# A Fourier filter beside an MLP mixer: the inverse length-47 set of one pair moved behind the forward set of the next pair

## The chip, the cores and the metric

The kernel runs on one core of one Trainium2 chip. The metric is the device time of one execution in microseconds (us). Three executions of the kernel before took 2443.66, 2444.45 and 2446.20 us; their median is 2444.45 us. All data are float32.

## What is computed

Two blocks follow each other. The first is a Fourier filter along a sequence of 3008 for each of 8 batches and 256 channels; the second is an MLP mixer on its result.

```python
X = np.fft.rfft(x, axis=1)                    # x: (8, 3008, 256)
Y = X * (filt_r + 1j * filt_i)[None]          # filt: (1505, 256)
y = np.fft.irfft(Y, n=3008, axis=1)

h = np.maximum(y.transpose(0, 2, 1) @ w_tok1, 0.0) @ w_tok2   # tokens, inner size 256
u = y + h.transpose(0, 2, 1)
out = u + np.maximum(u @ w_ch1, 0.0) @ w_ch2                  # channels, inner size 1536
```

## The kernel before

**The filter.** A length of 3008 is 64 times 47. The transform is done in two steps: a length-64 step ("a" units, `a_pair`) that writes its result to the DRAM tensor `z_tmp`, and a length-47 step that reads it. The length-47 step goes over 16 *pairs* of residues, numbered c. For each pair it does four things:

- `b_pair(c)`: the forward set. Four matmuls (`four`, L523), each on a 64x64 quarter of the array, from `t2` into the two PSUM banks named `acc` and `b` (the list `turn`). Then VectorE multiplies both banks by the filter (two instructions, L674) into the tiles `p1` and `p2`.
- `join(c)`: VectorE makes the complex product out of them in place in `p1` (L679, L680).
- `bi_pair(c)`: the inverse set. Four more quarter matmuls on L523 read `p1` and write two banks; ScalarE copies both out (`by_block`, L660) into `t3`, and two DMAs of the SyncE queue store it to `g_tmp` (L689).
- the loads of pair c+2 (`t2_load`, `w_load`), issued on the SyncE queue between the first two.

The pools around this: `p1` and `p2` have one buffer each, `t2` and `t3` two, the tables `wb` and the filter tiles three. The PSUM tag `pg` has two banks; every other tag has one.

**The batches.** `GROUPS` is (0), (1, 2), (3, 4), (5, 6), (7). The filter of the first group runs alone at the start. Each later group's filter runs beside the mixer of the group before it: `dft(GROUPS[1])` beside batch 0, `dft(GROUPS[2])` beside batches 1 and 2, and so on. Batch 7's mixer has nothing beside it. A group of two batches streams 512 columns in each quarter matmul, the last group, with one batch, 256.

**The mixer.** Its channel part is cut into 6 column tiles `m` of a batch and 6 inner blocks `jp` of each, together 36 *tiles* to a batch, in the order (m, jp). Both products use seven half-size multiplications instead of eight, so there are many small additions, most of which VectorE does. In each tile TensorE runs, in this order:

- `up_first` (L936): four matmuls into two new `pg` banks. ScalarE copies one quarter out (`s`, L939), then VectorE does `up_middle`: `u2` (written `hh<-ps_pg,s 128x256`) and then two sums into `s` (`s<-ps_pg,hh`).
- `down` part 0 of the tile before (L970, moving operand `hh`): three matmuls into the four `po` banks. Place 0 of the schedule follows.
- `up_last` (L952): three matmuls into the same `pg` banks. VectorE then adds both banks into `hh` (`hh<-ps_pg,s 128x512`, two instructions) and ScalarE applies the ReLU (L957). Place 1 follows.
- `down` part 1 of the tile before (L970, moving operand `t`): four matmuls on the sums t1, t3, t2, t4 in that order. VectorE makes these sums before (`h_sums`: one `t<-hh 128x512`, then two `t<-t,hh 128x256`). With the last `jp` of an m, `finish` is called here: VectorE adds the `po` banks into `u` and `r` over this and the next tiles. Place 2 follows.

Most matmuls are 128x128 by 256 columns. One such matmul is two passes in the profile, and a pass starts 0.216 us after the one before.

**Where the filter's steps go.** `mix` is a generator that stops at the places 0, 1 and 2 of every tile; at each stop the loop at the end of the kernel decides by `due` whether the filter's generator takes its next step. For the groups after the first, a forward set is due at place 1 of `jp` 5 and `jp` 2, `join` at place 1 of `jp` 0 and place 0 of `jp` 3, and an inverse set at place 0 of `jp` 1 and place 2 of `jp` 3. In the last m of a group the forward set is due at `jp` 1 instead of 2. Beside batch 0 there are only 36 tiles, so a forward set is due in most tiles, its `join` at place 2 of the same tile and its inverse set at place 0 of the next.

The order of each engine's instructions is the order in which the program emits them (`manual_schedule`); nothing is reordered later. A new tile in a buffer waits until every reader of the tile before it in that buffer is done.

Of the kernel before, what the change touches and what calls it, by code (L numbers as in the profile page):

```python
# [127 lines left out]
def kernel(  # L128
# [53 lines left out]
    def bank(tag):  # L182
        return (psg if tag == "pg" else psum).tile([P, 512], FP32, tag=tag, name="ps_" + tag)
# [341 lines left out]
    def half_of(half, n=HALF):  # L525
        return slice(half * HALF, half * HALF + n)
# [30 lines left out]
    def dft(bs):  # L557
# [102 lines left out]
            nc.scalar.copy(out=out.rearrange("p b (e g i) -> p b g e i", e=DH, i=CW),  # L660
                           in_=ps.rearrange("p b (g e i) -> p b g e i", e=DH, i=CW))

        def two_banks():
            return [bank(tag).rearrange("p (b d) -> p b d", b=2)[:, 0:nb, :] for tag in turn]

        def b_pair(c):
            pss, wb, t2 = two_banks(), wbs[c], t2s[c]
            four(lambda h, i: pss[h][half_of(i)], lambda h, i: wb[half_of(h, KH), i], lambda h, i: t2[half_of(h, KH), i])  # L670
            where = (p1p, p2p)
            for h in range(2):
                prods[c, h] = where[h].tile([P, 2, nb, D], FP32, tag="p%d" % (h + 1), name="p%d" % (h + 1))
                nc.vector.tensor_tensor(out=prods[c, h], in0=pss[h].unsqueeze(1).to_broadcast([P, 2, nb, D]),  # L674
                                        in1=filts[c % FB][:, :, 0, :].unsqueeze(2).to_broadcast([P, 2, nb, D]), op=ALU.mult)
# [3 lines left out]
            nc.vector.tensor_tensor(out=p1[:, 0], in0=p1[:, 0], in1=p2[:, 1], op=ALU.subtract)  # L679
            nc.vector.tensor_tensor(out=p1[:, 1], in0=p1[:, 1], in1=p2[:, 0], op=ALU.add)  # L680

        def bi_pair(c):
            pss, wb, p = two_banks(), wbs[c], prods.pop((c, 0))
            four(lambda i, h: pss[i][half_of(h)], lambda i, h: wb[half_of(i), 2 + h], lambda i, h: p[half_of(i), h])
            t3 = t3p.tile([P, KC, nb, D], FP32, tag="t3", name="t3")
            for i in range(KC):
                by_block(t3[:, i], pss[i])
            for h in range(2):
                nc.sync.dma_start(g_d[place_of[bs[0]][0]][ts(c, KC), ts(h, KH)].rearrange("k r b d -> r k b d"),  # L689
                                    t3[half_of(h, KH)])  # L690
# [8 lines left out]
        yield "w"  # L699
        yield "b"  # L700
        if not first:
            for c in range(K2 // KC):
                b_pair(c)
                if c + 2 < K2 // KC:
                    t2_load(c + 2)
                    w_load(c + 2)
                yield "m"
                join(c)
                yield "i"
                bi_pair(c)  # L710
                if c + 1 < K2 // KC:
                    yield "b"
            return
        if first:
            for i in range(2):
# [243 lines left out]
    def down(m, jp, part, hh, t, po):  # L959
        hw = width(m) // 2  # L960
        if not po:
            for i in range(4):
                po.append(bank("po%d" % i).rearrange("p (s n) -> p s n", s=2))
        b11, b21, b22 = (hh[:, i, 0:hw] for i in (0, 3, 2))
        t1, t3, t2, t4_ = (t[:, i, 0:hw] for i in range(4))

        todo = (((0, 0, 1, 0, 1, b21), (0, 1, 0, 1, 2, b22), (2, 0, 1, 0, 0, b11)),
                ((1, 1, 1, 0, 6, t1), (3, 0, 1, 1, 4, t3), (2, 1, 0, 1, 5, t2), (1, 0, 0, 1, 3, t4_)))
        for i, j, first, last, n, mov in todo[part]:
            nc.tensor.matmul(po[i][:, j, 0:hw], chan[1][:, jp, n, :], mov, start=(jp == 0 and first == 1),  # L970
                             stop=(jp == JP - 1 and last == 1))
# [74 lines left out]
    def mix(next_ready):  # L1046
# [31 lines left out]
        for i in range(len(items) + 1):  # L1078
# [50 lines left out]
            loads(b)  # L1129
            yield b, i % n, 1  # L1130
            if old:
                down(mo, jo, 1, hhs.pop(i - 1), tts.pop(i - 1), pos[bo, mo])
                if jo == JP - 1:
                    todo_v.extend(finish(bo, mo, uts[bo, mo], pos[bo, mo]))
                    one_step()
                    one_step()
# [16 lines left out]
    with tc.manual_schedule():  # L1153
# [70 lines left out]
        for b, i, place in mix(next_ready):  # L1224
            if group + 1 < len(GROUPS) and b == GROUPS[group + 1][0]:
                if not done:
                    raise AssertionError("the filter's steps don't fit beside the mixer's")
                group += 1
                done = group + 1 == len(GROUPS)
                todo = iter(()) if done else dft(GROUPS[group + 1]) if group else second  # L1230
                coming = "a"
            if done:
                continue
            jp = i % JP
            if coming in "aw":
                due = place == 1 or group == 0
            elif group:
                due = (jp, place) in {"b": ((5, 1), (1 if i >= n - JP else 2, 1)), "m": ((0, 1), (3, 0)), "i": ((1, 0), (3, 2))}[coming]
            else:
                due = (jp - (coming == "i")) % JP in ((5, 1, 2, 3) if i < 4 * JP else (5, 0, 1, 2, 3)) and place == {"b": 1, "m": 2, "i": 0}[coming]  # L1240
            if coming == "a" and group == 0 and i < JP - 1:
                due = (2, 0, 1)[place]
            for _ in range(due):
                if not done:
                    coming = next(todo, "end")
                    done = coming == "end"
# [30 lines left out]
```

## Time and profile before

The profiled execution took 2445.61 us, of which 2443.8 us are its span.

| what | value |
|---|---|
| median of three runs | 2444.45 us |
| profiled execution, span | 2445.61 us, 2443.8 us |
| TensorE granted clock, mean | 0.995 |
| VectorE, ScalarE, GpSimdE busy | 79%, 28%, 25% of the span |
| quarter matmuls on L523, forward and inverse sets | 128 sets: 96 of 512 columns, 32 of 256 |
| first forward set, last inverse set start at | 226.5 us, 2076.3 us |

The trace gives each instruction's start and duration from the span's start. A timeline row can hold several instructions of one kind: "x8" are eight, and the duration is then that of all of them together. A row of `L523` with `<-t` is part of a forward set, with `<-p` part of an inverse set. In square brackets stands how long the engine idled before the row and what ended the idling.

### The profile page before, as it was taken

How to read it: one execution, taken by the hardware profiler on the slowest of the kernel's cores; microseconds unless marked ns; L12 is line 12 of the kernel's file. 1: busy time of each engine (PE TensorE's matmuls, PEld its weight loads, DVE VectorE, ACT ScalarE, POOL GpSimd, SP SyncE). 2: the span in 40 equal slices, each digit the busy share in tenths (PEclk: the TensorE clock that was granted, in tenths of full speed). 3: DMA queues.
4: the chain of work that ended last, by engine and by line, in shares of the span. 5: the costliest groups of instructions: out<-in, count | busy, mean ns of one | idle time of the engine just before them, and what ended most of it. 6: DMA issues, size and time to landing. Idle time of an engine off the chain costs nothing.

```text
span 2443.8 us, 35574 instructions
## 1 busy us (share of the span) xinstructions
PE 2399.8 (98%) x12340; PEld 1971.9 (81%) x12340; DVE 1937.0 (79%) x3684; ACT 687.0 (28%) x1355; POOL 621.0 (25%) x1115
## 2 busy tenths in 40 slices
PE   7999999999999999999999999999999999999998
PEld 4666676978788877987888878897889888898887
DVE  7798788787887788778878887877787787777776
ACT  5733223132222222123222222213221222212222
POOL 7476332122112211211211122112112112112121
PEclk8999999999999999999999999999999999999999
DMA  9985446453352222445344322433324121411100
GB/s 215 249 231 170 147 148 180 157 160 108 113 150 90 74 86 79 158 128 158 97 118 122 87 81 73 156 96 118 101 78 149 50 72 47 148 62 31 38 15 20
DMA packets 187419, 278.65 MB, mean 114 GB/s; under 512 B 35485, under 2 KB 125291, under 8 KB 187240
## 3 DMA queue, kind: packets, MB, share of 16 engines
q1 hardware_dynamic: 140952, 212.56, 29.1%
q0 software_dynamic: 34688, 53.83, 8.2%
q10 hardware_dynamic: 11600, 10.00, 1.3%
q8 instruction: 98, 1.61, 0.3%
q14 instruction: 81, 0.66, 0.1%
HBM read 193.52 MB, written 82.72 MB: 113 GB/s over the span
## 4 chain that ended last, share of the span: by engine, by line
PE 88%; DVE 6%; DMA 3%; issue 1%; ACT 1%; POOL 0%; SPq 0%; ACTq 0%; DVEq 0%; POOLq 0%
PE ps_po L970 33%; PE ps_pg L936 18%; PE ps_pg L952 14%; PE ps_b L523 5%; PE ps_b L802 3%; PE ps_acc L857 3%; PE ps_acc L802 2%; PE ps_b L857 2%; PE ps_b L835 2%; PE ps_acc L835 2%; DVE t L914 1%; PE ps_acc L523 1%; PE ps_b L751 1%; DVE hh L914 1%; DMA st<-in_moe_w_tok_dram 1%
## 5 line engine op out<-in xcount | busy, mean ns | idle before, releaser
L1017 POOL DMA_DIRECT2D out_dram<-r x752 | 408.2, 550 | 1636.0 <-ACT hh L957 1157.1
L914 DVE TENSOR_TENSOR hh<-ps_pg,s 128x512 f32<-128x512 f32 (+3 forms) x864 | 481.6, 585 | 230.7 <-ACT s L939 227.9
L957 ACT ACTIVATE hh<-hh 128x512 f32<-128x512 f32 (+1 forms) x576 | 347.7, 621 | 951.0 <-DVE hh L914 947.1
L970 PE MATMUL ps_po<-t,wc 128*128 128x256 f32 (+1 forms) x2304 | 546.8, 380 | 5.0 <-DVE t L914 4.0
L970 PEld LDWEIGHTS ps_po<-t,wc 128*128 128x128 f32 x2304 | 426.4, 190 | 130.9 <-DVE t L914 45.1
L970 PE MATMUL ps_po<-hh,wc 128*128 128x256 f32 (+1 forms) x1728 | 414.0, 375 | 1.4 <-POOL wc L382 0.8
L936 PE MATMUL ps_pg<-v,wc 128*128 128x256 f32 (+1 forms) x1728 | 413.4, 375 | 0.2 <-DVE v L914 0.2
L970 PEld LDWEIGHTS ps_po<-hh,wc 128*128 128x128 f32 x1728 | 326.5, 190 | 42.9 <-ACT s L939 3.4
L936 PEld LDWEIGHTS ps_pg<-v,wc 128*128 128x128 f32 x1728 | 326.8, 190 | 40.9 <-DVE v L914 3.2
L952 PE MATMUL ps_pg<-u,wc 128*128 128x256 f32 (+1 forms) x1152 | 295.2, 379 | 0.6 <-DVE hh L914 0.4
L952 PEld LDWEIGHTS ps_pg<-u,wc 128*128 128x128 f32 x1152 | 214.9, 190 | 57.5 <-DVE hh L914 25.8
L914 DVE TENSOR_TENSOR t<-t,hh 128x256 f32<-128x256 f32 (+1 forms) x576 | 244.9, 425 | 19.8
L914 DVE TENSOR_TENSOR s<-ps_pg,hh 128x512 f32<-128x512 f32 (+1 forms) x288 | 196.0, 681 | 30.7 <-DVE hh L914 0.9
L939 ACT COPY s<-ps_pg 128x256 f32<-128x256 f32 (+1 forms) x288 | 105.9, 368 | 335.5 <-PE ps_pg L936 332.5
L914 DVE TENSOR_TENSOR t<-hh 128x512 f32<-128x512 f32 (+1 forms) x288 | 194.0, 674 | 0.6 <-ACT hh L957 0.6
L936 PE MATMUL ps_pg<-u,wc 128*128 128x256 f32 (+1 forms) x576 | 171.8, 380 | 3.4 <-DVE hh L914 3.4
L952 PE MATMUL ps_pg<-v,wc 128*128 128x256 f32 (+1 forms) x576 | 168.8, 375 | 0.0
L936 PEld LDWEIGHTS ps_pg<-u,wc 128*128 128x128 f32 x576 | 106.2, 190 | 35.1 <-DVE hh L914 20.1
L914 DVE TENSOR_TENSOR u<-ps_acc,u 128x256 f32<-128x256 f32 (+1 forms) x84 | 46.2, 549 | 94.0 <-PE ps_acc L857 86.6
L952 PEld LDWEIGHTS ps_pg<-v,wc 128*128 128x128 f32 x576 | 109.2, 190 | 12.6
L914 DVE TENSOR_TENSOR u<-ps_b,u 128x512 f32<-128x512 f32 (+2 forms) x126 | 74.4, 591 | 28.9 <-PE ps_b L857 26.7
L857 PE MATMUL ps_acc<-w 128*128 128x256 f32 (+1 forms) x336 | 85.2, 376 | 0.0
(149 smaller groups left out, 2718.0 us busy)
## 6 DMA issues: line engine op xcount, KB each, us to landing
w<-w_tmp SPq DMA_DIRECT2D x84, 448.0 KB
w<-w_tmp SPq DMA_DIRECT2D x35, 896.0 KB
out_dram<-r POOLq DMA_DIRECT2D x696, 32.0 KB, 3.3
t<-g_tmp SPq DMA_DIRECT2D x42, 512.0 KB
g_tmp<-t SPq DMA_DIRECT2D x96, 192.0 KB
t<-z_tmp SPq DMA_DIRECT2D x180, 96.0 KB
z_tmp<-t SPq DMA_DIRECT2D x60, 256.0 KB
filt<-in_x_dram SPq DMA_DIRECT2D x90, 128.0 KB
```

Of the source, the lines that this page charges most:

```text
L523: nc.tensor.matmul(outs(i, j), stat(i, j), mov(i, j), start=True, stop=True)
L751: nc.tensor.matmul(acc[:, t, :], w1[:, a, ts(t, P)], t4[b, a // TC4][:, a % TC4, :], start=(a == 0 and t == 0), stop=(a == A - 1 and t == ...
L802: nc.tensor.matmul(ps[:, at], w[:, n], mov, start=(j == 0 and i in (0, 2)), stop=(j == AP - 1 and i >= 5))
L835: nc.tensor.matmul(ps[:, ds(q * P, n)], t4[b, c][:, r, ts(dh, P)], wai[:, 0:n], start=(first and q == 0), stop=(not first and q == 3))
L857: nc.tensor.matmul(ps[:, ds(j * hw, hw)], h1[:, n, :], w2m[m % 2][:, at, 0:hw], start=(i < 2 and j == 0), stop=(j == len(todo) - 1))
L914: nc.vector.tensor_tensor(out=out, in0=in0, in1=in1, op=op)
L936: nc.tensor.matmul(ps[:, 0:hw], chan[0][:, jp, n, :], mov, start=True, stop=True)
L939: nc.scalar.copy(out=s[:, 0], in_=g[0][:, 0, 0:hw])
L952: nc.tensor.matmul(ps[:, 0:hw], chan[0][:, jp, n, :], mov, start=True, stop=True)
L957: nc.scalar.activation(out=hs, in_=hs, func=AF.Relu)
L970: nc.tensor.matmul(po[i][:, j, 0:hw], chan[1][:, jp, n, :], mov, start=(jp == 0 and first == 1), stop=(jp == JP - 1 and last == 1))
L1017: q.dma_start(bass.AP(tensor=ob.tensor, offset=ob.offset + row * D + g * cw, ap=[[N1 * D, 32], [D if h else -D, n], [1, cw]]), blocks[ts(g ...
```

## The change

A forward set is now followed at once by the inverse set of the pair before, and both stand in the middle of `down` part 1 rather than ahead of it. The inverse set takes the two `pg` banks (those of the tile's own up product) instead of `acc` and `b`. Only the last inverse set of a group stays on its own, at its old place and in its old banks. `down` part 1 is split into two parts of two matmuls, with a new place 1.5 between them. The filter's VectorE multiplication is split off into `products` and is emitted behind the inverse set.

```diff
-        def two_banks():
-            return [bank(tag).rearrange("p (b d) -> p b d", b=2)[:, 0:nb, :] for tag in turn]
+        def two_banks(tags):
+            return [bank(tag).rearrange("p (b d) -> p b d", b=2)[:, 0:nb, :] for tag in tags]
...
         def b_pair(c):
-            pss, wb, t2 = two_banks(), wbs[c], t2s[c]
+            pss, wb, t2 = two_banks(turn), wbs[c], t2s[c]
             four(lambda h, i: pss[h][half_of(i)], lambda h, i: wb[half_of(h, KH), i], lambda h, i: t2[half_of(h, KH), i])
+            return pss
+
+        def products(c, pss):
             where = (p1p, p2p)
...
-        def bi_pair(c):
-            pss, wb, p = two_banks(), wbs[c], prods.pop((c, 0))
+        def bi_pair(c, tags):
+            pss, wb, p = two_banks(tags), wbs[c], prods.pop((c, 0))
...
-            for c in range(K2 // KC):
-                b_pair(c)
-                if c + 2 < K2 // KC:
+            last = K2 // KC
+            for c in range(last):
+                pss = b_pair(c)
+                if c:
+                    bi_pair(c - 1, ("pg", "pg"))
+                products(c, pss)
+                if c + 2 < last:
                     t2_load(c + 2)
                     w_load(c + 2)
                 yield "m"
                 join(c)
-                yield "i"
-                bi_pair(c)
-                if c + 1 < K2 // KC:
-                    yield "b"
+                yield "b" if c + 1 < last else "i"
+            bi_pair(last - 1, turn)
             return
...
         todo = (((0, 0, 1, 0, 1, b21), (0, 1, 0, 1, 2, b22), (2, 0, 1, 0, 0, b11)),
-                ((1, 1, 1, 0, 6, t1), (3, 0, 1, 1, 4, t3), (2, 1, 0, 1, 5, t2), (1, 0, 0, 1, 3, t4_)))
+                ((1, 1, 1, 0, 6, t1), (3, 0, 1, 1, 4, t3)), ((2, 1, 0, 1, 5, t2), (1, 0, 0, 1, 3, t4_)))
...
             if old:
-                down(mo, jo, 1, hhs.pop(i - 1), tts.pop(i - 1), pos[bo, mo])
+                down(mo, jo, 1, hhs[i - 1], tts[i - 1], pos[bo, mo])
+            yield b, i % n, 1.5
+            if old:
+                down(mo, jo, 2, hhs.pop(i - 1), tts.pop(i - 1), pos[bo, mo])
                 if jo == JP - 1:
...
-                due = (jp, place) in {"b": ((5, 1), (1 if i >= n - JP else 2, 1)), "m": ((0, 1), (3, 0)), "i": ((1, 0), (3, 2))}[coming]
+                due = (jp, place) in {"b": ((5, 1.5), (1 if i >= n - JP else 2, 1.5)), "m": ((0, 1), (3, 0)), "i": ((1, 0), (3, 2))}[coming]
             else:
-                due = (jp - (coming == "i")) % JP in ((5, 1, 2, 3) if i < 4 * JP else (5, 0, 1, 2, 3)) and place == {"b": 1, "m": 2, "i": 0}[coming]
+                due = (jp - (coming == "i")) % JP in ((5, 1, 2, 3) if i < 4 * JP else (5, 0, 1, 2, 3)) and place == {"b": 1.5, "m": 2, "i": 0}[coming]
```

The number of matmuls, VectorE and ScalarE instructions and DMAs stays the same. In each of the four later groups 15 inverse sets move behind a forward set, 60 in all.

More of the change, by code (lines that the diff above doesn't have):

```diff
@@ L1235 @@
             if coming in "aw":
-                due = place == 1 or group == 0
+                due = place == 1 or group == 0 and place != 1.5
             elif group:
-                due = (jp, place) in {"b": ((5, 1), (1 if i >= n - JP else 2, 1)), "m": ((0, 1), (3, 0)), "i": ((1, 0), (3, 2))}[coming]
+                due = (jp, place) in {"b": ((5, 1.5), (1 if i >= n - JP else 2, 1.5)), "m": ((0, 1), (3, 0)), "i": ((1, 0), (3, 2))}[coming]
             else:
-                due = (jp - (coming == "i")) % JP in ((5, 1, 2, 3) if i < 4 * JP else (5, 0, 1, 2, 3)) and place == {"b": 1, "m": 2, "i": 0}[coming]
+                due = (jp - (coming == "i")) % JP in ((5, 1, 2, 3) if i < 4 * JP else (5, 0, 1, 2, 3)) and place == {"b": 1.5, "m": 2, "i": 0}[coming]
             if coming == "a" and group == 0 and i < JP - 1:
-                due = (2, 0, 1)[place]
+                due = {0: 2, 1: 0, 1.5: 0, 2: 1}[place]
             for _ in range(due):
```

## The prediction

> **What bounds the kernel now.** I read the page first: busy shares, then the chain of waits.
>
> ```profile
> PE 2399.8 (98%) x12340; PEld 1971.9 (81%) x12340; DVE 1937.0 (79%) x3684; ACT 687.0 (28%) x1355; POOL 621.0 (25%) x1115
> ...
> PE 88%; DVE 6%; DMA 3%; issue 1%; ACT 1%; POOL 0%; SPq 0%; ACTq 0%; DVEq 0%; POOLq 0%
> ```
>
> TensorE is busy 98% of the span and carries 88% of the chain. Only less TensorE time, or less waiting of TensorE, can help. VectorE's 79% is a mean; whether it has slack where the change acts, only the timeline says. So I read the timeline of TensorE and VectorE around one forward set and the inverse set that follows (batches 1 and 2):
>
> ```profile
> 1192.13 0.59 PE L952 MATMUL ps_pg<-v,wc 128*128 128x256 f32 x2
> 1192.65 0.65 PE L523 MATMUL ps_b<-t,wb 48*64 48x512 f32 x2
> 1193.13 0.60 PE L523 MATMUL ps_b<-t,wb 48*64 48x512 f32 x2
> 1193.67 1.99 PE L970 MATMUL ps_po<-t,wc 128*128 128x256 f32 x8
> ...
> 1199.82 1.89 PE L970 MATMUL ps_po<-t,wc 128*128 128x256 f32 x8
> ...
> 1204.74 0.65 PE L523 MATMUL ps_b<-p,wb 64*64 64x512 f32 x2
> 1205.76 1.13 PE L952 MATMUL ps_pg<-u,wc 128*128 128x256 f32 x4
> 1207.27 1.96 PE L970 MATMUL ps_po<-t,wc 128*128 128x256 f32 x8
> ```
>
> And VectorE over the same stretch:
>
> ```profile
> 1194.22 0.87 DVE L914 TENSOR_TENSOR v<-v,u 128x256 f32<-128x256 f32 x2
> 1195.13 1.22 DVE L674 TENSOR_TENSOR p<-ps_b,filt 128x1024 f32<-128x1024 f32 x1
> 1196.28 1.21 DVE L674 TENSOR_TENSOR p<-ps_acc,filt 128x1024 f32<-128x1024 f32 x1
> 1197.41 0.41 DVE L914 TENSOR_TENSOR hh<-ps_pg,s 128x256 f32<-128x256 f32 x1
> ...
> 1204.65 0.41 DVE L914 TENSOR_TENSOR hh<-ps_pg,s 128x256 f32<-128x256 f32 x1
> ...
> 1206.44 0.68 DVE L914 TENSOR_TENSOR t<-hh 128x512 f32<-128x512 f32 x1
> ```
>
> See two things. The L970 row behind the set takes 1.99 where an undisturbed one takes 1.89. And VectorE runs back to back from 1194.2 to the end of `t<-hh` at 1207.12, in the rows left out too (none of them waits over 0.15); `down` part 1 starts 0.15 later, at 1207.27. Over these 12 us VectorE is as late as TensorE.
>
> Beside batch 0 VectorE is already late:
>
> ```profile
> 375.12 0.68 DVE L679 TENSOR_TENSOR p<-p,p 128x512 f32<-128x512 f32 x1
> ...
> 375.95 1.15 PE L523 MATMUL ps_b<-p,wb 64*64 64x512 f32 x3 [0.44 <-DVE p L679]
> ...
> 377.47 1.13 PE L952 MATMUL ps_pg<-u,wc 128*128 128x256 f32 x4
> ```
>
> The inverse set starts late for `join`, and L952 comes 1.52 after it instead of 1.02.
>
> **What the Trainium skill says.** "TensorEngine Tiling (Array Packing)", Key Properties: changing the tiling mode drains TensorE, and different tiles work in parallel. The trace agrees: four quarter matmuls start within 0.02 us of each other, and a set has a gap ahead and behind. "TensorE: Matmul & The Clock Gate", its opening table, calls VectorE's queue strict FIFO, so a waiting multiplication holds all behind it. Its text on LDWEIGHTS says weights are pulled ahead into the background buffer; the trace agrees inside a set (second pass 0.48 after the first). No run yet shows it between two sets.
>
> **Part 1: TensorE alone.** A pass of 256 columns lasts 0.216. L952's two passes from 1192.13 end at 1192.56; the set starts at 1192.65 (0.09), the next matmul 1.02 later, and its row loses 0.10. A set alone costs 0.09+1.02+0.10 = 1.21. Right behind another it should add two passes of 0.48 = 0.96: 0.25 saved. With 256 columns (1767.69 to 1768.28 in the timeline, second pass 0.26 after the first): 0.09+0.59+0.10 = 0.78 against 0.53, again 0.25. 60 x 0.25 = 15.2 us saved, were nothing else late. If the second set's weights aren't pulled ahead, 0.13 (one load's duration) of the 0.25 is gone; if its passes run at 0.43 (512 columns at 0.84 ns), 0.10 more is saved. I take 0.25.
>
> **Part 2: the multiplication now waits for the inverse set.** `p1` has one buffer. The inverse set of pair c-1 reads it, and `products(c)` overwrites it. Before, that set was long done; now it stands just ahead, and both multiplications and all of VectorE's queue (`u2`, `s`, the sums t, `hh`) wait for its last matmul. Let T be the forward set's start before. Now t1, t3 come first (four passes, 0.86), then passes at +0, +0.48, +0.96, +1.44 of the merged sets; the last is issued 0.02 later, lasts 0.59, and about 0.05 later the reader starts. So the multiplication starts at T+0.86+1.46+0.59+0.05 = T+2.96. Before it started at T+2.4 to T+2.5 at `jp` 5 (1195.13), T+2.2 at `jp` 2, and as early as T+1.2 beside batch 0 (340.89 to 342.09).
>
> **Part 3: what that costs at each place.**
>
> Batches 1 to 4 (two-batch filters of groups 2 and 3). At `jp` 5: `u2` also waits for ScalarE's `s`, which follows `up_first`, 0.96 later than before; `u2` starts at 1197.97 instead of 1197.41, +0.56. VectorE has no gap to make this up, so L970 of `jp` 1 starts at 1207.27+0.56. The inverse set that is gone from `jp` 1 was cover: without it TensorE reaches L970 early and waits for `t<-hh`. A loss of 0.56. At `jp` 2 TensorE is the later one: the timeline shows VectorE idle 2.3 us before `u2` two tiles on, so removing the set at `jp` 3 pays in full: -0.26. Two pairs: +0.30.
> A group: first pair 0 (nothing added at `jp` 5, nothing gained at `jp` 1), the next -0.26, five such couples +1.5, the couple across `jp` 5/`jp` 1 of the last m +0.67 (VectorE +1.31 by the transposes there, then 0.64 back at the inverse set that waited 0.47 for `join`), one more `jp` 5 +0.56, and the last forward set +0.96, as its group's last inverse set stays: +3.4. Two groups: +6.9.
>
> Batches 5, 6 (256 columns): multiplications of 0.69, and the set ends before VectorE is ready, so only the +0.53 through `s` matters: +0.24 at `jp` 5, -0.25 at `jp` 2. With first and last pair +0.5 for the group.
>
> Batch 0: forward sets in consecutive tiles. The loop closes: multiplications 2.27, join 1.2, `u2` and gap 0.5, `s` 0.6, `t<-hh` 0.68 and its 0.15, t1/t3 and entry 0.95, 2.1 to the next multiplication = 8.5 us, against 8.62 between forward sets before (332.27, 340.89). A transpose (0.63) or `finish` (2.3) in the loop adds itself.
> Worked for the m whose first set starts at 308.43, as delay of the multiplication. `jp` 5: T+2.96 against T+2.41, +0.55. `jp` 1: `t<-hh` ended at 323.40 and is 0.55 late; t1 0.15 behind it, 0.95 to the merged sets, 2.10 to the multiplication: 327.15 against 326.04, +1.11. Before, the forward set stood ahead of t1 and hid this wait. `jp` 2 in the same way, behind a transpose: 336.34 against 334.69, +1.65. `jp` 3: 344.91 against 342.09, +2.82. `jp` 4 has no set: `t<-hh` ends 2.82 late, L970 starts at 350.46 against 349.28, +1.18; from there TensorE is the later one again.
> Over the whole batch: -1.2 at pair 0, whose successor's tile loses its inverse set and gains none; +1.9, +1.2, +3.2 over the next three m (the last has `jp` 0 too, where `finish` stands in the loop; the joins' waits above, 4.9 us in all, go in this sum); +0.96 for the last set. Sum +6.1; every term hangs on VectorE's order, so -2 to +10.
>
> **Cheap parts.** The inverse set waits until VectorE has read both `pg` banks: at 1194.30, and it wants them from T+1.82 = 1194.47. The cover is 0.17; gone, it costs its lateness per tile. ScalarE's two copies (0.59 each) end by the set's start +3.1, and `up_first` writes the second bank at +3.8, the first at +2.95 when copy one ended at +2.65: nothing, else up to 0.3. On SyncE the two stores to `g_tmp` now stand ahead of pair c+2's 13 loads and wait for these copies, about 1 us; the loads are wanted two pairs on (17 us beside batch 0, 40 later): nothing. POOL's queue is passed by nothing.
>
> **Sum.** 6.9+0.5+6.1 = +13.5 us on the profiled execution's 2445.61; that is 1.2 above the median. On the median 2444.45 this gives **2458 us**.
>
> **Rivals.**
> - *TensorE's account decides* (faster). VectorE makes up its delay, because 79% busy leaves slack: -15.2 us, 2429; with some of batch 0's 4.9 us of waits gone 2424. For it: TensorE's 98%. Against: the gapless VectorE rows to 1207.12. It decides if L970 of `jp` 1 isn't late.
> - *A draw.* VectorE's delay is half of what I sum (the multiplication starts at T+2.7, or batch 0 comes out even): +6.9 falls to about 3, 6.1 to 0, 2444 to 2449.
> - *The pair isn't back to back.* The inverse set waits for `pg`, or `up_first` for the copies, 0.3 in each of 60 tiles: 18 us more, 2476. The single 0.17 of cover speaks for it.
>
> **Chances.** Forecast 0.68 (own range 2449 to 2468), TensorE's account 0.14, draw 0.12, worse 0.06. A measurement tells 0.2%, 4.9 us, from no change. Faster 0.15, same 0.14, slower 0.71. The range 2438 to 2470 leaves out most of the first rival and the last.
>
> **What would show it.** Right: L523 rows `<-t` and `<-p` adjacent with 0.48 between passes; VectorE idle before L677 (old L674) until the set's end; L970 of `jp` 1 waiting for `t`; batches 5 and 6 unchanged within 1 us. Wrong: VectorE not waiting at L677, TensorE's busy time unchanged while the span falls, or idle time at `up_first` for ScalarE.

## The result, and the profile after

The changed kernel takes 2459.97 us (median of four runs, 2458.07 to 2464.33), against 2445.32 us for the kernel before on the same chip (four runs, 2443.66 to 2447.88). The ratio is 1.0061, 95% interval 1.0044 to 1.0079: slower by 14.65 us. The profiled execution took 2458.07 us, its span is 2456.3 us.

Two lines of the page of after: busy times, then the shares of the chain of waits. The third is the group of the seven-product's `down` part with the sums t, now on L975, with its idle time at the end.

```profile
PE 2392.6 (97%) x12340; PEld 1979.5 (81%) x12340; DVE 1941.0 (79%) x3684; ACT 686.1 (28%) x1355; POOL 622.4 (25%) x1115
...
PE 42%; DVE 8%; issue 1%; DMA 0%; ACT 0%; SPq 0%; DVEq 0%; ACTq 0%; POOL 0%
...
L975 PE MATMUL ps_po<-t,wc 128*128 128x256 f32 (+1 forms) x2304 | 559.6, 381 | 19.9 <-DVE t L919 18.9
```

The same group on the page of before:

```profile
L970 PE MATMUL ps_po<-t,wc 128*128 128x256 f32 (+1 forms) x2304 | 546.8, 380 | 5.0 <-DVE t L914 4.0
```

TensorE is busy for 7.2 us less than before (2399.8), so the sets did become cheaper; by more than this, since part of the waiting is counted as busy (the rows of the inverse set grow while it waits for its `pg` banks, as shown below). Yet the span is 12.5 us longer. Of the 19.7 us in which TensorE newly does nothing, 14.9 stand ahead of this one group (19.9 less 5.0), and they wait for VectorE's sums. The chain's shares add up to about half of the span only (it was not followed further back), so they are not to be set against those of before.

The view of waits of after names what is new or has grown (before, TensorE's rows of `down` waited 4.0 us for t, in 9 waits, and the other two lines are absent but for one wait of 0.2 for a forward set). The columns are the idle time in us, how often, and the longest:

```profile
DVE p L677 <- PE ps_pg L523: 25.2, 42, 1.2
...
PEld ps_pg L523 <- DVE hh L919: 19.6, 81, 0.3
PE ps_po L975 <- DVE t L919: 18.9, 37, 0.6
```

The multiplication (L677) waits for the inverse set's last matmul; the inverse set's weight loads wait until VectorE has read the `pg` banks; `down` waits for t. Most of the waits of the second line delay no matmul: one of them, of 0.22, ends at 1244.49 in the place shown next, and the matmul comes at its usual distance, at 1244.56. What they cost is read from the matmuls, below.

Next, one forward set at `jp` 5 and the tiles behind it, at the same place of the work in both traces. It lies beside batches 3 and 4 (so did the rows of the prediction from 1192, which its text put beside batches 1 and 2; the order is the same in both). TensorE after:

```profile
1243.65 0.65 PE L523 MATMUL ps_b<-t,wb 48*64 48x512 f32 x2
...
1244.13 0.60 PE L523 MATMUL ps_b<-t,wb 48*64 48x512 f32 x2
1244.15 0.59 PE L523 MATMUL ps_acc<-t,wb 48*64 48x512 f32 x2
1244.56 1.04 PE L523 MATMUL ps_pg<-p,wb 64*64 64x512 f32 x8
1245.53 1.13 PE L975 MATMUL ps_po<-t,wc 128*128 128x256 f32 x4
...
1256.71 0.59 PE L957 MATMUL ps_pg<-v,wc 128*128 128x256 f32 x2
1257.90 1.96 PE L975 MATMUL ps_po<-t,wc 128*128 128x256 f32 x8 [0.59 <-DVE t L919]
```

The forward passes start at 1243.65 and 1244.13, the inverse ones 0.43 behind (1244.56), and the next ordinary matmul 1.88 after the first. A set alone takes 1.02 to that point, so the second adds 0.86. VectorE after:

```profile
1244.36 0.88 DVE L919 TENSOR_TENSOR v<-v,u 128x256 f32<-128x256 f32 x2
1245.75 1.23 DVE L677 TENSOR_TENSOR p<-ps_b,filt 128x1024 f32<-128x1024 f32 x1 [0.52 <-PE ps_pg L523]
1246.89 1.22 DVE L677 TENSOR_TENSOR p<-ps_acc,filt 128x1024 f32<-128x1024 f32 x1
1248.03 0.42 DVE L919 TENSOR_TENSOR hh<-ps_pg,s 128x256 f32<-128x256 f32 x1
...
1257.07 0.68 DVE L919 TENSOR_TENSOR t<-hh 128x512 f32<-128x512 f32 x1
```

And VectorE before, at the same place of the work:

```profile
1240.42 0.87 DVE L914 TENSOR_TENSOR v<-v,u 128x256 f32<-128x256 f32 x2
1241.33 1.23 DVE L674 TENSOR_TENSOR p<-ps_b,filt 128x1024 f32<-128x1024 f32 x1
1242.47 1.22 DVE L674 TENSOR_TENSOR p<-ps_acc,filt 128x1024 f32<-128x1024 f32 x1
1243.61 0.41 DVE L914 TENSOR_TENSOR hh<-ps_pg,s 128x256 f32<-128x256 f32 x1
...
1252.64 0.68 DVE L914 TENSOR_TENSOR t<-hh 128x512 f32<-128x512 f32 x1
```

The after trace stands 3.94 later here (`v<-v,u` at 1244.36 and 1240.42). Taking that off, the multiplication starts 0.48 late, `u2` 0.48, `t<-hh` 0.49. The row of L975 that needs it waits 0.59 by the profile; by the starts it comes 0.76 later than the two passes of L957 ahead of it take (1256.71 to 1257.90, less 0.43).

To see where the span grew I cut each trace, one of each kernel, at the same instructions: for every later group from the last matmul of the up product ahead of its first forward set to the first quarter set of the next group's length-64 step (for the last group to its last inverse set). What lies outside is the same work in all kernels, but the time at which the first stretch starts moves between 222.6 and 227.7 us from profile to profile without any relation to the edits. So the stretches are compared, and the medians beside them. Where kernels have the same order beside batches 1 to 6, their stretches agree within 0.1; beside batch 0 three kernels with the order of after differ by up to 1.2 (272.36 to 273.53), so a difference of 1 there says little.

| stretch, us | before | after | difference | forecast |
|---|---|---|---|---|
| batch 0 | 267.26 | 272.53 | +5.3 | +6.1 |
| batches 1, 2 | 459.36 | 462.02 | +2.7 | +3.4 |
| batches 3, 4 | 459.62 | 462.03 | +2.4 | +3.4 |
| batches 5, 6 | 353.63 | 359.30 | +5.7 | +0.5 |
| sum | | | +16.0 | +13.5 |

The profiled after reached the start of its first stretch 3.7 earlier than the profiled before did, so its span shows 12.5 of these 16.0.

The same cut can be made tile by tile, from one `up_first` to the next. Beside batches 3 and 4 an undisturbed tile takes 6.04 in both kernels, and a lone set adds 1.21 or 1.22. In after, a tile with two sets takes 0.86 more than the same tile with its forward set took before. A tile at `jp` 3 and the next one, which lose an inverse set, give back 1.21 together. But of the tiles at `jp` 1 that lose theirs the first gives back nothing, and the six others outside the batch's last m only 0.28 to 0.58: in a usual m such a tile took 7.45 before (0.2 of it waiting) and takes 7.16 after (1.12 of it waiting). So a couple of `jp` 5 and `jp` 1 loses 0.28 to 0.58, and one of `jp` 2 and `jp` 3 gains 0.35. (The last m that has its own places in `due` is that of each batch, since `i` counts within a batch.)

### The profile page after: what moved, and what is told of

Same layout as the page of the kernel before. It is cut to its first block, busy times and chain, and to the rows that moved or that the text cites. A ratio compares the mean times of both kernels' runs of the same rounds, so it can differ in the third digit from the quotient of the medians.

```text
span 2456.3 us, 35588 instructions
## 1 busy us (share of the span) xinstructions
PE 2392.6 (97%) x12340; PEld 1979.5 (81%) x12340; DVE 1941.0 (79%) x3684; ACT 686.1 (28%) x1355; POOL 622.4 (25%) x1115
## 4 chain that ended last, share of the span: by engine, by line
PE 42%; DVE 8%; issue 1%; DMA 0%; ACT 0%; SPq 0%; DVEq 0%; ACTq 0%; POOL 0%
PE ps_po L975 16%; PE ps_pg L941 9%; PE ps_pg L957 6%; PE ps_acc L862 2%; PE ps_b L807 2%; DVE t L919 2%; DVE u L919 2%; PE ps_b L862 1%; PE ps_acc L807 1%; PE ps_b L523 1%; DVE hh L919 1%; DVE s L919 1%; PE ps_pg L523 1%; PE ps_b L840 1%; PE ps_acc L840 1%
## 5 line engine op out<-in xcount | busy, mean ns | idle before, releaser
L975 PE MATMUL ps_po<-t,wc 128*128 128x256 f32 (+1 forms) x2304 | 559.6, 381 | 19.9 <-DVE t L919 18.9
L975 PEld LDWEIGHTS ps_po<-t,wc 128*128 128x128 f32 x2304 | 424.0, 190 | 154.2 <-issue 55.4
L975 PE MATMUL ps_po<-hh,wc 128*128 128x256 f32 (+1 forms) x1728 | 413.4, 375 | 1.3 <-POOL wc L382 0.8
L975 PEld LDWEIGHTS ps_po<-hh,wc 128*128 128x128 f32 x1728 | 327.4, 190 | 40.7 <-POOL wc L382 2.1
L957 PE MATMUL ps_pg<-u,wc 128*128 128x256 f32 (+1 forms) x1152 | 294.7, 378 | 4.9 <-DVE hh L919 3.7
L957 PEld LDWEIGHTS ps_pg<-u,wc 128*128 128x128 f32 x1152 | 215.4, 190 | 47.1 <-DVE hh L919 22.1
L957 PE MATMUL ps_pg<-v,wc 128*128 128x256 f32 (+1 forms) x576 | 168.8, 375 | 0.0
L957 PEld LDWEIGHTS ps_pg<-v,wc 128*128 128x128 f32 x576 | 108.7, 190 | 13.1
L677 DVE TENSOR_TENSOR p<-ps_b,filt 128x1024 f32<-128x1024 f32 (+1 forms) x64 | 69.8, 1091 | 30.1 <-PE ps_pg L523 25.2
```

What stands on the lines that cost most here:

```text
L957: nc.tensor.matmul(ps[:, 0:hw], chan[0][:, jp, n, :], mov, start=True, stop=True)
```

## The experiments

The ratios are to runs of before made together with each experiment: 17 runs with a median of 2445.41 us for the first four kernels, 13 runs with 2445.53 for the other four.

The theory I held after this: VectorE gets `t` late in groups 2 and 3 and in batch 0, for two reasons (the multiplication waits for the inverse set through `p1`, and `up_first` and with it `s` come later), and the inverse set no longer fills TensorE's time at `jp` 1; beside batches 5 and 6 the inverse set waits for its `pg` banks. The rivals: the place in the middle of `down` costs the time, or VectorE's load as such.

**The other product first.** `p2` is not read by the inverse set. With it first, one multiplication of 1.2 us covers the wait for `p1`:

```diff
-            for h in range(2):
+            for h in (1, 0):
```

> The changed kernel with one order turned round: of the two filter multiplications the one into p2 is issued first. It needs only the forward set; the one into p1 still waits for the inverse set. Theory (VectorE stands idle behind the single p1 buffer, and beside batch 0 the loop through it is longer than TensorE's work): VectorE is given 1.1 us of the wait back. Beside batch 0 the loop falls from about 8.4 to 7.3 us, under TensorE's 8.0, and the stretch from the first forward set to the next group's first length-64 set falls from 272.2 us to 258 to 266. At jp 5 of batches 1 to 4 nothing is won, because u2 waits for ScalarE's s copy as well (in the changed kernel it ends at 1247.99, the multiplications at 1248.1), so L975 of jp 1 stays 0.4 to 0.5 late; batches 5 and 6 unchanged. Total 2447 to 2453. Rival one (VectorE has simply too much to do, its order doesn't matter): 2460 within 3. Rival two (the waits of the inverse set for its pg banks are the loss): 2460 within 3.

Measured 2452.58 us (six runs, 2451.61 to 2454.69), ratio to before 1.0031 (1.0019 to 1.0043), 7.4 us under after. The stretch of batch 0 is 265.88, that is 6.65 less than after and 1.4 less than before; the others are unchanged within 0.4 (461.67, 461.66, 359.22). Both the total and the stretch lie just inside what was expected. VectorE of after in batch 0, from one multiplication to the next:

```profile
324.10 1.23 DVE L677 TENSOR_TENSOR p<-ps_b,filt 128x1024 f32<-128x1024 f32 x1 [0.58 <-PE ps_pg L523]
325.24 1.22 DVE L677 TENSOR_TENSOR p<-ps_acc,filt 128x1024 f32<-128x1024 f32 x1
326.49 0.69 DVE L682 TENSOR_TENSOR p<-p,p 128x512 f32<-128x512 f32 x1
...
333.40 1.23 DVE L677 TENSOR_TENSOR p<-ps_b,filt 128x1024 f32<-128x1024 f32 x1 [0.56 <-PE ps_pg L523]
```

With `p2` first:

```profile
321.76 1.21 DVE L677 TENSOR_TENSOR p<-ps_acc,filt 128x1024 f32<-128x1024 f32 x1
322.90 1.21 DVE L677 TENSOR_TENSOR p<-ps_b,filt 128x1024 f32<-128x1024 f32 x1
324.14 0.69 DVE L682 TENSOR_TENSOR p<-p,p 128x512 f32<-128x512 f32 x1
...
330.42 1.18 DVE L677 TENSOR_TENSOR p<-ps_acc,filt 128x1024 f32<-128x1024 f32 x1
```

The same loop, with the same transposes in it, takes 9.30 with the wait and 8.66 without. Without transposes it was 8.71 and is 8.12, which is what TensorE's own work in a tile with two sets takes where nothing waits. So in batch 0 the wait for `p1` makes the loss. The waits for the `pg` banks are the smaller part there: in after they lengthen 12 of the 15 moved inverse sets by 0.12 to 0.19, 2.0 in all, and with `p2` first they are still there, about 2.3 in nine sets. In groups 2 and 3 the wait for `p1` is gone too and next to nothing is gained, since `u2` is then held by ScalarE's `s` just as long:

```profile
1239.36 1.23 DVE L677 TENSOR_TENSOR p<-ps_acc,filt 128x1024 f32<-128x1024 f32 x1
1240.50 1.21 DVE L677 TENSOR_TENSOR p<-ps_b,filt 128x1024 f32<-128x1024 f32 x1
1242.11 0.42 DVE L919 TENSOR_TENSOR hh<-ps_pg,s 128x256 f32<-128x256 f32 x1 [0.39 <-ACT s L944]
```

This is the place shown above (`v<-v,u` starts at 1238.44 here); `u2` follows `v<-v,u` by 3.67, as in after (1244.36 to 1248.03). In after the two conditions of `u2` are met within 0.1 of each other (the `s` copy of 0.37 starts at 1247.62, the second multiplication ends near 1248.1), so removing one leaves the other.

**The middle of `down` alone.** The forward set stands where the change puts it; the inverse set stays alone at its old place, in its old banks.

```diff
-                pss = b_pair(c)
-                if c:
-                    bi_pair(c - 1, ("pg", "pg"))
-                products(c, pss)
+                products(c, b_pair(c))
...
-                yield "b" if c + 1 < last else "i"
-            bi_pair(last - 1, turn)
+                yield "i"
+                bi_pair(c, turn)
+                if c + 1 < last:
+                    yield "b"
```

> The kernel before with one part of the change: every forward set in the middle of down part 1, every inverse set alone at its old place and in its old banks. Theory: batches 1 to 6 take the same time as before (within 1 us each), because the forward set only changes places with two matmuls and the multiplication starts at or before the time at which VectorE is ready; beside batch 0, where VectorE took some multiplications 1.2 us after the set started, up to 4 us are lost. Total 2444 to 2450. Rival (the place in the middle, where t1 is no longer covered by the set, costs the time): 2455 or more, with L975 of the forward set's own tile waiting for t.

Measured 2446.12 us (twelve runs, 2444.57 to 2449.80), ratio 1.0005 (0.9997 to 1.0014). Batch 0 takes 1.4 more than before, the other three stretches are equal to before within 0.2. The place by itself is not the cause; the 1.4 in batch 0 is hardly more than the differences between profiles there.

**VectorE's load.** Two kernels leave the two instructions of `join` out, so the complex product is not formed and p1 goes into the inverse set as the multiplication left it; one is made from before, one from after.

```diff
-            p1, p2 = prods[c, 0], prods.pop((c, 1))
-            nc.vector.tensor_tensor(out=p1[:, 0], in0=p1[:, 0], in1=p2[:, 1], op=ALU.subtract)
-            nc.vector.tensor_tensor(out=p1[:, 1], in0=p1[:, 1], in1=p2[:, 0], op=ALU.add)
+            prods.pop((c, 1))
```

> The kernel before without join, that is without the two VectorE additions that make the complex product of each pair (1.2 us of VectorE's time for each of the 64 pairs; the inverse sets then read the uncombined products). A measure for the next run. Theory: TensorE is the bound nearly everywhere, so only its waits for VectorE go, most of them beside batch 0 (4.9 us at the inverse sets): 2435 to 2442. If VectorE's amount of work were the bound as a whole, it would fall by far more, towards 2400.

> The changed kernel without join in the same way. Theory: with 1.2 us of slack per pair VectorE no longer passes its delay on, L975 of jp 1 doesn't wait, and TensorE's own account shows: 60 times 0.35 us won at the merged sets (as the changed kernel's trace has it: a merged pair takes 0.86 more than a set alone, which takes 1.21), less about 8 us of waits of the inverse set for its pg banks (0.39 in each of 15 tiles beside batches 5 and 6, 0.15 in some 12 beside batch 0). So it is faster than before_nojoin, by 7 to 15 us: 2422 to 2433. Rival (the pg banks, ScalarE's copies or the split of down part 1 are what costs, and VectorE's lateness is only a sign of it): it stays slower than before_nojoin, by 5 us or more.

Measured 2434.52 us for the one made from before (four runs; ratio to before 0.9953, 0.9937 to 0.9970), half a us below the expected range, and 2434.05 for the one made from after (four runs; 0.9952, 0.9937 to 0.9967). The two are equal: the change's loss is gone, but the gain that I expected of it without `join` didn't come, and my theory was half right here. By stretch, after without `join` against before without it: batch 0 -0.9, the two-batch groups -1.4 and -1.7, batches 5 and 6 +3.5. The group of the multiplication in after without `join`:

```profile
L677 DVE TENSOR_TENSOR p<-ps_b,filt 128x1024 f32<-128x1024 f32 (+1 forms) x64 | 69.8, 1090 | 34.6 <-PE ps_pg L523 31.1
```

It waits 31.1 us for the inverse set, more than after's 25.2: a VectorE with less to do is only earlier at the same wait. Beside batches 3 and 4 the waits of `down` for t between L955 and L973, summed from TensorE's timeline, grow from 0.6 in before without `join` to 3.6. By tile, the one at `jp` 1 takes 7.26 in before without `join`, with its inverse set and without waiting, and 6.39 in after without it, of which 0.35 is waiting; it gives back 0.87 where the pair at `jp` 5 costs 0.86, so such a couple comes out even. So VectorE's load is not the whole cause: with a lighter VectorE the new order still makes t late, though by less (1.12 of waiting with `join`). The +3.5 of batches 5 and 6 come with waits for the `pg` banks, 5.7 us there, which leaving `join` out doesn't touch.

**The pair only where its delay is harmless.** In groups 2 and 3 the inverse set of every second pair, the one due at `jp` 3, runs behind the forward set at `jp` 5. The other stays at `jp` 1, where it fills TensorE's time until t is there. All other sets are as before. (The last line of the cut is the part of the `due` table that is new; `"B"` is a forward set at its old place.)

```diff
+        def behind_next(c):
+            return bs in GROUPS[2:4] and c % 2 == 1
...
                 pss = b_pair(c)
-                if c:
-                    bi_pair(c - 1, ("pg", "pg"))
+                if held is not None:
+                    bi_pair(held, ("pg", "pg"))
...
-                yield "b" if c + 1 < last else "i"
-            bi_pair(last - 1, turn)
+                held = c if c + 1 < last and behind_next(c) else None
+                if held is None:
+                    yield "i"
+                    bi_pair(c, turn)
+                if c + 1 < last:
+                    yield "b" if held is not None else "B"
...
+                        "B": ((5, 1), (1 if i >= n - JP else 2, 1)),
```

> The inverse set is moved behind the next forward set only in the filters of batches 3, 4 and of 5, 6, and only where that forward set is at jp 5; the inverse sets of jp 1 stay alone, and batch 0 and batches 5, 6 have the old order. So 7 inverse sets a group move, all from the end of jp 3. Theory: at jp 1 the inverse set is cover for VectorE's lateness and costs nothing to keep; at jp 3 VectorE has slack, so 1.21 us go there and 0.86 come at jp 5. TensorE, not VectorE (0.5 late), is then the later one at jp 1. Each move wins 0.35 (one of them up to 0.5 more, where the set waited for join): the stretches of these two groups, 459.4 and 459.6 us before, become 456 to 457.5; the others stay as before. Total 2438 to 2442. Rival one (every set merged this way costs, whatever it leaves behind): the two stretches grow, by 7 times 0.5, total 2449 or more. Rival two (TensorE wins nothing by back-to-back sets): total 2445 within 2.

Measured 2439.80 us (five runs, 2435.91 to 2440.72), ratio 0.9971 (0.9959 to 0.9983): faster than before. The stretches of groups 2 and 3 fall to 455.97 and 455.97, by 3.4 and 3.65; batch 0 and batches 5, 6 are those of before within 0.15. Seven sets are moved in each group. TensorE of this kernel at the place shown above, at `jp` 5 and at the `jp` 1 that follows:

```profile
1232.64 0.60 PE L523 MATMUL ps_b<-t,wb 48*64 48x512 f32 x2
1232.66 0.60 PE L523 MATMUL ps_acc<-t,wb 48*64 48x512 f32 x2
1233.07 1.04 PE L523 MATMUL ps_pg<-p,wb 64*64 64x512 f32 x8
...
1244.17 0.65 PE L523 MATMUL ps_b<-p,wb 64*64 64x512 f32 x2
...
1246.16 0.59 PE L965 MATMUL ps_pg<-v,wc 128*128 128x256 f32 x2
1246.59 1.67 PE L983 MATMUL ps_po<-t,wc 128*128 128x256 f32 x7
```

And its VectorE:

```profile
1234.26 1.23 DVE L677 TENSOR_TENSOR p<-ps_b,filt 128x1024 f32<-128x1024 f32 x1 [0.52 <-PE ps_pg L523]
...
1245.57 0.69 DVE L927 TENSOR_TENSOR t<-hh 128x512 f32<-128x512 f32 x1
```

VectorE waits the same 0.52 at the multiplication, and `t<-hh` follows it by 11.31, as in after (1245.75 to 1257.07). It is just as late. But L983 follows L965 after 0.43, two passes, with no wait: the inverse set at 1244.17 stands in that time. Summed beside batches 3 and 4 in the timeline, TensorE's gaps between `up_last` and `down` part 1 are 1.8 us before, 6.7 after and 1.3 here. It is the set taken away from `jp` 1 that turns VectorE's lateness into TensorE's. By tile, the 3.65 beside batches 3 and 4 are made up so: six of the moved sets bring 0.35 each, 2.1; the seventh, in the batch's last m, costs 0.39, because the tile that it leaves gives back only 0.47; and the seven tiles at `jp` 1 become 0.18 to 0.47 shorter, 1.9 in all, although they keep their sets. Before, TensorE waited for t by that much in each of them (7.45 instead of 7.26 in a usual m); now it comes there 0.86 later and VectorE only 0.5, and the wait is gone. So half of the gain is not in the cheaper sets.

**A later place beside batches 5 and 6.** There the sets go behind three of the four matmuls of `down` part 1 instead of two, so that VectorE has read the `pg` banks. (`k` is the new argument of `down`, 2 elsewhere; its second call is changed in the same way.)

```diff
+        todo = (todo[0], todo[1][0:k], todo[1][k:])
...
-                down(mo, jo, 1, hhs[i - 1], tts[i - 1], pos[bo, mo])
+                down(mo, jo, 1, hhs[i - 1], tts[i - 1], pos[bo, mo], 3 if bo in GROUPS[3] else 2)
```

> The changed kernel, but beside batches 5 and 6 the two sets stand behind three of the four matmuls of down part 1 instead of behind two. Theory: with 256 columns the forward set is short (0.53 us less the gap), so the inverse set reaches its second pg bank 0.39 us before VectorE has read it; that wait is the 5 us that the forecast for this group lacked. One matmul (0.43) more ahead of the sets takes it away, as the reads don't get later: the stretch of this group, 359.3 us in the changed kernel and 353.6 before, becomes 352.5 to 355.5. The other stretches don't change, total 2453 to 2457. Rival (VectorE waits for s and passes it on, as at batches 1 to 4, or up_first now waits for ScalarE's copies): 358 or more, total as the changed kernel's.

Measured 2456.62 us (four runs, 2456.28 to 2457.00), ratio 1.0042 (1.0028 to 1.0056). The stretch falls from 359.30 to 355.49, of before's 353.63. TensorE of after at such a place, from the second round of the forward set on:

```profile
1775.33 0.38 PE L523 MATMUL ps_b<-t,wb 48*64 48x256 f32 x2
...
1775.55 1.01 PE L523 MATMUL ps_pg<-p,wb 64*64 64x256 f32 x8
1776.49 1.13 PE L975 MATMUL ps_po<-t,wc 128*128 128x256 f32 x4
```

The inverse set's weight loads there, and then VectorE's read of the two `pg` banks:

```profile
1775.33 0.36 PEld L523 LDWEIGHTS ps_pg<-p,wb 64*64 64x64 f32 x4
1775.91 0.19 PEld L523 LDWEIGHTS ps_pg<-p,wb 64*64 64x64 f32 x4 [0.22 <-DVE hh L919]
```

```profile
1774.57 1.28 DVE L919 TENSOR_TENSOR hh<-ps_pg,s 128x512 f32<-128x512 f32 x2
```

The read ends at 1775.85, and the loads for the second bank's quarters follow at 1775.91. And TensorE with the later place:

```profile
1777.49 0.38 PE L523 MATMUL ps_b<-t,wb 48*64 48x256 f32 x2
...
1777.71 0.61 PE L523 MATMUL ps_pg<-p,wb 64*64 64x256 f32 x8
1778.25 0.70 PE L976 MATMUL ps_po<-t,wc 128*128 128x256 f32 x2
```

The inverse set takes 1.01 here where it waits and 0.61 where it doesn't. In after 14 of the 15 sets beside these batches wait, by 0.33 to 0.45, 5.5 in all; with the later place 0.15 is left of that, and 3.8 come off the stretch. What eats part of the rest is a wait on the other side: with one matmul left between, `up_first` finds the banks still being copied by ScalarE. In that kernel's waits beside these two batches:

```profile
PEld ps_pg L941 <- ACT t L660: 3.2, 14, 0.2
```

These are waits of weight loads; the matmuls behind them start 0.10 late in each tile, 1.4 in all (from the timeline).

**`join` later.** In groups 2, 3 and 4, except in a batch's last m, `join` goes from place 1 of `jp` 0 to place 2 of `jp` 1, behind the sums that `jp` 1 waits for. (Only the changed part of the `due` line is shown.)

```diff
-  "m": ((0, 1), (3, 0))
+  "m": ((0, 1) if i >= n - JP else (1, 2), (3, 0))
```

> The changed kernel with one VectorE job moved: the join of the pair whose forward set is at jp 5 is due at place 2 of jp 1 instead of place 1 of jp 0 (outside batch 0 and a group's last m). Theory: between the multiplications at jp 5 and t of jp 1 VectorE has no gap, and join is 1.2 us of that chain; without it L975 of jp 1 no longer waits (0.76 beside batches 1 to 4, 0.50 beside batches 5, 6), and in its new place, behind t and hh of jp 1, VectorE has 0.7 us of idle time, so about 0.2 us are lost at jp 2. So the stretches of groups 2 and 3 fall from 462.0 to 456.5 to 459, that of group 4 from 359.3 to 355.5 to 358, batch 0 stays at 272.5 within 2. Total 2445 to 2453. Rival (the lost cover at jp 1 costs in any order, or the wait of the multiplication for the inverse set is what counts): stretches unchanged within 1 us, total 2458 or more.

Measured 2454.41 us (seven runs, 2451.26 to 2456.50), ratio 1.0031 (1.0020 to 1.0042), which is 5.6 under after and 1.4 above the expected range. The stretches themselves came as expected: 458.91 for both two-batch groups (-3.1 each) and 357.84 (-1.5). Most of what is over lies in batch 0, which this edit doesn't touch (273.53 against 272.53). By tile, 0.3 of that 1.0 stand in the tile of the first pair and 0.7 in two later tiles, where the inverse set waits for its `pg` banks by 0.39 and 0.18; why VectorE reads them later there stays open. The wait for t beside batches 3 and 4, summed from the timeline for L957 to L975, falls from 6.7 to 4.0 us but doesn't vanish: `join`'s 1.2 us were part of what made `jp` 1 late, and the delay from `jp` 5 remains. By tile, `jp` 1 becomes 0.76 shorter in a usual m (7.16 to 6.40), and the pair's tile at `jp` 2 0.32 longer, 0.18 of it because the inverse set now waits for its `pg` banks there too. VectorE's time is moved rather than won.

**What pays, together.** In batch 0 all inverse sets behind the next forward set, with `p2` first; in groups 2 and 3 only those behind `jp` 5; beside batches 5 and 6 the old order. The cut is against the kernel with the pair at `jp` 5 only; `p2` comes first in all groups.

```diff
-            return bs in GROUPS[2:4] and c % 2 == 1
+            return bs == GROUPS[1] or bs in GROUPS[2:4] and c % 2 == 1
...
-            for h in range(2):
+            for h in (1, 0):
```

> A version meant to be faster than both kernels: beside batch 0 the changed order with the multiplication into p2 first, in groups 2 and 3 the inverse set moved only where the forward set is at jp 5, beside batches 5 and 6 the old order. Theory: the parts add up as their stretches say: batch 0 265.9 (as with p2 first), groups 2 and 3 456 to 457.5, group 4 353.6, that is 7 us less than before, 2436 to 2441. Rival (the parts don't add up, since the time at which each stretch starts shifts DMAs and copies): 2443 or more.

Measured 2435.93 us (five runs, 2435.12 to 2437.07), ratio to before 0.9958 (0.9946 to 0.9971): 9.6 us faster than the before of the same round and 24 faster than the change as it was made. The stretches are 266.04, 455.89, 455.90 and 353.63, together 8.4 less than before. The total lies at the lower edge of what was expected, so the parts add up.

The stretches of all kernels, in us:

| kernel | median, us | batch 0 | 1, 2 | 3, 4 | 5, 6 |
|---|---|---|---|---|---|
| before | 2445.32 | 267.26 | 459.36 | 459.62 | 353.63 |
| after | 2459.97 | 272.53 | 462.02 | 462.03 | 359.30 |
| other product first | 2452.58 | 265.88 | 461.67 | 461.66 | 359.22 |
| middle alone | 2446.12 | 268.65 | 459.33 | 459.59 | 353.79 |
| before, no `join` | 2434.52 | 262.09 | 456.40 | 456.40 | 353.63 |
| after, no `join` | 2434.05 | 261.20 | 455.00 | 454.67 | 357.12 |
| pair at `jp` 5 only | 2439.80 | 267.13 | 455.97 | 455.97 | 353.63 |
| later place, batches 5, 6 | 2456.62 | 272.36 | 462.05 | 462.04 | 355.49 |
| `join` later | 2454.41 | 273.53 | 458.91 | 458.91 | 357.84 |
| together | 2435.93 | 266.04 | 455.89 | 455.90 | 353.63 |

A second buffer for `p1`, which would take that wait away altogether, was not tried.

## Why the prediction was right, and where a term was off

The forecast of 2458 and the measured 2459.97 lie 2 us apart. In batch 0 and in groups 2 and 3 the reason given is the one that the runs show; beside batches 5 and 6, where 5.7 of the 16.0 us were lost, it is another. The nearness of the two numbers is partly luck: one term was 5 us too small, three were 2.5 us too large together, and the two medians of before differ by 0.9.

- **Part 1.** The second set was to add 0.96 and save 0.25 (60 of these are 15.0, not 15.2); it adds 0.86 and saves 0.35, because its passes follow at 0.43. With 256 columns it adds 0.43 instead of 0.53 where it doesn't wait. The text had named this case, though its sign of being right, 0.48 between passes, didn't come. It is worth 60 x 0.10 = 6 us of TensorE's time, but little of it reaches the span, since where VectorE is late TensorE waits that much longer.
- **Part 2.** The multiplication was to start at T+2.96. The set starts 0.86 after T, so T is 1242.79 in the timeline above and the multiplication's 1245.75 is T+2.96. That it fits to the digit is luck: the passes follow 0.10 faster than was taken, and from the end of the set (1245.60) to the reader it is 0.15 instead of 0.05. At most other places of groups 2 and 3 it is 0.09, which gives T+2.91.
- **Part 3, groups 2 and 3.** `down` of `jp` 1 was to start 0.56 late; it starts 0.49 late, and the kernel that keeps the inverse set at `jp` 1 shows that the missing cover turns this into lost time. By tile a couple of `jp` 5 and `jp` 1 loses 0.28 to 0.58 (0.56 was forecast), one of `jp` 2 and `jp` 3 gains 0.35 (0.26), the first pair changes nothing (0) and the last forward set costs 0.86 (0.96). The groups lose 2.7 and 2.4 instead of 3.4, in keeping with sets that are 0.10 cheaper. What the text didn't name is that TensorE already waited 0.2 to 0.5 for t at each `jp` 1 before. The reason the text gave for `u2`, the later `s`, also holds: with `p2` first the wait for `p1` goes and these stretches don't change.
- **Batch 0.** A loop of 8.5 plus 0.63 for a transpose was forecast, 9.30 was measured, and the stretch grew by 5.3 against +6.1. With the wait for `p1` taken out it falls to 265.88, a little below before's. The 2.0 of waits for the `pg` banks in it were not in the sum.
- **Batches 5 and 6: the mis-sized term.** +0.5 was forecast, +5.7 measured. The step is in the cheap parts: the cover of 0.17 between VectorE's last read of the `pg` banks and the inverse set was worked out for 512 columns and taken for all places. With 256 columns the forward set's two passes take 0.53 instead of 0.96, so the banks are wanted 0.43 sooner, and the cover is 0.17 - 0.43 = -0.26. In the trace above the read ends at 1775.85 and the second bank is wanted at 1775.56, 0.01 behind the first matmul of the set: -0.29. Such a wait was priced at its lateness; measured, the set ends 0.40 later there, and 14 of 15 sets wait. The sign that the text gave for this group, unchanged within 1 us, failed. The later place takes 3.8 of the 5.7 off; of the 1.9 left, 1.4 is that place's own wait of `up_first` for ScalarE's copies. The remaining 0.5 is as large as the forecast for this group without the bank wait.
- **The other cheap parts.** Costing ScalarE's copies at nothing held in after; the price of 0.1 per tile with the later place lies inside the bound of 0.3. Costing SyncE's loads at nothing held too. The profile puts two waits of the multiplication in after down to a load (0.60 each), but both end 0.09 behind the inverse set's end, like the waits put down to that set; and where it names a load for a forward set, the gap is the 0.33 that stands ahead of the other forward sets as well.
- **The rivals.** That VectorE makes up its delay is refuted by the row of L975 at `jp` 1; TensorE's busy time did fall, by 7.2, without any gain. The draw is refuted too: beside batches 1 to 4 the multiplication starts at T+2.9 or later, not T+2.7, and batch 0 doesn't come out even. That the pair isn't back to back is true where the inverse set waits for `pg`: in 14 tiles beside batches 5 and 6, by 0.33 to 0.45, and in 12 beside batch 0, by 0.12 to 0.19. Beside batches 1 to 4 no moved set waits by more than 0.03.

## What to carry to other kernels

Before a piece of TensorE work is moved to save its set-up, ask what it stood in front of: here the inverse set at `jp` 1 filled a time in which TensorE would have waited anyway, and only the sets that cover nothing are worth moving. Where two pieces are put back to back, look at what the second reads or overwrites that somebody else wants next: reordering two independent VectorE instructions was worth 7 us. A margin worked out for one size of operand (0.17 us at 512 columns) has to be worked out again for each other size; at 256 it was negative (-0.29).

## What the runs showed of the hardware that was not expected

Inside a lone set of 512 columns the second round of quarter matmuls starts 0.48 us after the first, but where nothing waits all later rounds of two sets in a row start 0.43 to 0.44 apart, with other weights, another moving operand and other banks. The Trainium skill ("TensorE: Matmul & The Clock Gate", the text on LDWEIGHTS) says that weight loads are pulled ahead of matmuls in flight; the trace now agrees between two sets as well: in after, the inverse set's first weight loads are recorded at 1775.33, at the start of the forward set's second round, and its first matmul at 1775.55.

In these traces a wait of a matmul for the PSUM bank that it will write is recorded on its weight load. Where the inverse set waits for VectorE's read of a `pg` bank, the bracket stands behind the loads at 1775.91; the row of the eight matmuls only grows from 0.61 to 1.01 and shows no wait.
